# One PSUM tile of eight banks with the kernel's own lists, and an output projection in row halves, in a pre-LayerNorm attention and SwiGLU block

## The chip, the core and the metric

The kernel runs on one core of one Trainium2 chip. The core has a matrix engine (TensorE, in the profile PE for matmuls and PEld for weight loads), a vector engine (VectorE, DVE), a scalar engine (ScalarE, ACT), a general engine (GpSimd, POOL) and a queue that issues transfers (SyncE, SP). Matmul results land in PSUM, which has 128 partitions and eight banks of 512 float32 values per partition; VectorE and ScalarE read them out. The metric is the device time of one execution in microseconds, lower is better.

## The reference

One sequence of 2048 tokens and 640 channels goes through attention with 32 heads of 20 channels and through a SwiGLU feed-forward with 1728 hidden units; both have a LayerNorm without weights in front and a residual around.

```python
def _A_ref(x, wqkv, wo):
    qkv = ((x @ wqkv).reshape(B, S, 3, H, Dh)).transpose(2, 0, 3, 1, 4)
    q, k, v = qkv[0], qkv[1], qkv[2]
    scores = jnp.einsum("bhqd,bhkd->bhqk", q, k) * (Dh ** -0.5)
    p = _softmax(scores, axis=-1)
    o = jnp.einsum("bhqk,bhkd->bhqd", p, v)
    return o.transpose(0, 2, 1, 3).reshape(B, S, D) @ wo
def _B_ref(x, w_gate, w_up, w_down):
    return (_silu(x @ w_gate) * (x @ w_up)) @ w_down
h  = x + _A_ref(_layernorm(x), A_wqkv, A_wo)
h2 = h + _B_ref(_layernorm(h), B_w_gate, B_w_up, B_w_down)
```

## The kernel before

The program is one straight list of instructions, unrolled in Python. The order on each engine is the order in which the code calls them; a framework adds the waits between engines. Most float32 operands are split into a high and a low part (`split`, line 87: a copy on ScalarE, a subtraction on another engine), and a product is taken as hi*hi + hi*lo + lo*hi.

**PSUM.** In each stage the kernel opens a pool of PSUM tiles, and closes it before the next. A pool gives tiles of one name in a ring: the next tile of a name waits until the one that held the same buffer has been read for the last time. The first tiles of a new pool lie where tiles of the old pool lay. The four pools are:

- `psum_f` (line 70), for the first token flips: three `ps_wide` of two banks, one `ps_one`;
- `psum` (line 871), for the input projection: three `ps_one`, five `ps_single`;
- `psum_a` (line 995), for attention: four `ps_one` (scores), three `ps_max`, one `acc`;
- `psum2` (line 1494), for the feed-forward: four `ps_b`, four `ps_a`.

**Stage 1, to 328 us.** Tokens are normalised, transposed by TensorE (`flip_tokens`, line 759, and `flip`, line 739) and multiplied with wqkv. The first two blocks of output (`first_blocks`, line 781; products at line 788) use whole 128-row products. All later ones run as jobs of a planner (`Halves`, line 514): a job goes through its 15 products once with the upper 64 rows of the contraction and once with the lower 64 (`issue`, line 547; products at 556), so two jobs can use the two row halves of the array at the same time. In between it places products for the maxima of the scores (lines 186 and 210). The planner keeps its own clock and reckons when banks come free; its order does not depend on the profile.

**Stage 2, 328 to 1470 us: attention.** A unit is one group of four heads and one chunk of 512 queries; there are 32 (`NU`), 0 to 31, and each has 16 steps `kt`, one for each 128 keys. A step follows a string such as `"sMsSmSmW"` (line 43). `s` and `S` are score products, in the lower and upper row half (`scores`, line 1331, product 1336, exponential by ScalarE at 1342). `m` and `M` are products for the maxima of later units, again in row halves (`max_one`, line 225, product 229, reduced by VectorE at 235). `W` weighs the values with the exponentials of the step before (`weigh`, line 1344, product 1346, into `acc`, in column tiles of 32); after it, one entry of the list `extra` is run. When no maxima are left, the string is `"sSsSW"`. At the end of a unit `acc` is copied out (`row_sums`, line 1354, copy at 1356).

The output projection is cut by query chunk (`projection`, line 1038). In the last two units, 30 and 31, `extra` holds the projection of chunk 0 and of chunk 1: in steps 0 to 7 one half-projection each (`project`, line 1063: 15 products of 128 rows at line 1070 into one bank of `ps_max`, added to h by VectorE at line 1076, statistics at 1077 and 1079), in steps 8 to 10 the LayerNorm factors, in steps 12 to 15 a transpose with its split (`flip`, line 1095, products at 1102). Chunks 2 and 3 are projected after attention, from `ps_b`.

**Stage 3, 1470 us to the end.** Projections 2 and 3, and the feed-forward: `products` (line 1510, product 1514) into `ps_a`, and the down projection (`multiply`, line 1605, product 1608) into `ps_b`.

## Time and profile before

| what | value |
|---|---|
| time, median of 3 runs | 2038.6 us (2038.28 to 2039.58) |
| the profiled execution's own time | 2035.66 us |
| its span, first to last instruction | 2033.9 us |
| mean granted TensorE clock | 0.997 |
| PE busy, PEld busy | 99%, 61% of the span |
| DVE, ACT, POOL busy | 79%, 72%, 39% |

A row of the profile in order of time gives the start and duration in microseconds, the engine, the line, the operation, the tile written and those read, and the shape; in square brackets stands how long the engine was idle before, and what ended that. Matmuls are pipelined and their ends are modelled, so rows of PE overlap, and a busy PE is not PE at its peak. `L88` and `L89` are the two halves of the helper `split`.

### The profile page before, as it was taken

Reading aid. Unit: us, or ns where it says so; the run is one execution under the profiler, and the core shown is the slowest. Engines: PE = TensorE matmul, PEld = TensorE weight load, DVE = VectorE, ACT = ScalarE, POOL = GpSimd, SP = SyncE. Lnnn points to the kernel's source line nnn. Section 1 sums busy time; section 2 is a strip of 40 time slices with the busy share of each in tenths; the row PEclk is TensorE's granted clock in tenths of the full one; section 3 lists DMA queues with packets and bytes.
Section 4 is the critical chain, followed back from the end, with each engine's and each line's share of the span. In section 5 each row is a group of like instructions: output and inputs, shape, how many; then the busy total and the mean of one; then the engine's idle time right before and its main releaser. Section 6 shows DMA issues by size and latency. Waiting matters only on the chain. (4 is left out here: it accounts for less than half of the span.)

```text
span 2033.9 us, 39129 instructions
## 1 busy us (share of the span) xinstructions
PE 2008.8 (99%) x13716; PEld 1238.9 (61%) x13716; DVE 1612.6 (79%) x3241; ACT 1462.4 (72%) x2952; POOL 785.7 (39%) x1079
## 2 busy tenths in 40 slices
PE   7999999999999999999999999999999999999999
PEld 6899996333333333333333333345598888888888
DVE  6678788888888888888888888885377666676677
ACT  3788988999999999999999999987633222211221
POOL 5554450334434334344430011011145454744555
PEclk9999999999999999999999999999999999999999
DMA  7776663343443534444433123211158654974642
GB/s 227 243 222 186 203 185 100 113 128 99 150 124 113 163 123 138 129 141 146 141 126 109 30 65 80 83 62 49 41 193 292 222 193 156 346 272 159 202 151 95
DMA packets 205124, 305.03 MB, mean 150 GB/s; under 512 B 47664, under 2 KB 82480, under 8 KB 203904
## 3 DMA queue, kind: packets, MB, share of 16 engines
q1 hardware_dynamic: 204832, 302.53, 45.9%
q8 instruction: 109, 1.79, 0.4%
q14 instruction: 87, 0.71, 0.1%
q10 hardware_dynamic: 96, 0.00, 0.0%
HBM read 205.78 MB, written 95.68 MB: 148 GB/s over the span
## 5 line engine op out<-in xcount | busy, mean ns | idle before, releaser
L1342 ACT ACTIVATE probs<-ps_one 128x512 f32<-128x512 f32 x2048 | 1056.9, 615 | 62.0 <-PE ps_one L1336 24.2
L235 DVE TENSOR_REDUCE mx<-ps_max 128x1 f32<-128x512 f32 x1472 | 925.4, 684 | 116.2 <-PE ps_max L229 64.1
L1336 PE MATMUL ps_one<-q_stk,k_stk 62*128 62x512 f32 x2048 | 583.5, 431 | 1.2 <-DVE mx L199 1.2
L1346 PE MATMUL acc<-probs,v_stk 128*32 128x512 f32 x4096 | 546.7, 605 | 0.0
L229 PE MATMUL ps_max<-k_stk,q_stk 60*128 60x512 f32 x1472 | 488.7, 440 | 0.1
L1336 PEld LDWEIGHTS ps_one<-q_stk,k_stk 62*128 62x128 f32 x2048 | 290.5, 185 | 284.7 <-ACT probs L1342 269.7
L229 PEld LDWEIGHTS ps_max<-k_stk,q_stk 60*128 60x128 f32 x1472 | 245.2, 185 | 165.4 <-DVE mx L235 126.9
L1729 DVE TENSOR_TENSOR tmp<-ps_a,tmp 128x512 f32<-128x512 f32 x208 | 141.3, 690 | 122.1 <-PE ps_a L1514 96.4
L1346 PEld LDWEIGHTS acc<-probs,v_stk 128*32 128x32 f32 x4096 | 80.6, 108 | 181.7 <-issue 169.5
L1608 PE MATMUL ps_b<-halves,yp 128*128 128x320 f32 x1032 | 179.0, 308 | 1.5 <-POOL yp L89 1.3
L1608 PEld LDWEIGHTS ps_b<-halves,yp 128*128 128x128 f32 x1032 | 165.2, 188 | 17.5 <-POOL yp L89 1.5
L1514 PE MATMUL ps_a<-t,units 128*128 128x512 f32 x624 | 162.5, 396 | 0.0
L246 POOL CAST both<-neg 128x16 fp32r<-128x16 f32 x32 | 6.6, 207 | 361.6 <-PE ps_one L1336 153.7
L1514 PE MATMUL ps_a<-z,units 128*128 128x512 f32 x516 | 133.9, 394 | 0.0
L89 POOL TENSOR_TENSOR yp<-y,yp 128x256 fp32r<-128x256 f32 x96 | 60.2, 627 | 189.8 <-ACT yp L88 189.8
L1514 PEld LDWEIGHTS ps_a<-t,units 128*128 128x128 f32 x624 | 112.6, 188 | 18.5
L1613 DVE TENSOR_TENSOR h<-ps_b,h 128x320 f32<-128x320 f32 x248 | 110.0, 482 | 6.9 <-PE ps_b L1608 5.4
L216 DVE CUSTOM_DVE_ANT_0 q_stk<-ps_single,q_stk 128x512 f32<-128x512 f32 x143 | 95.7, 689 | 22.4 <-ACT q_stk L222 15.0
L1514 PEld LDWEIGHTS ps_a<-z,units 128*128 128x128 f32 x516 | 93.1, 187 | 16.0
L556 PE MATMUL ps_one<-z_hi,w_hi 64*128 64x512 f32 x380 | 99.1, 402 | 1.8 <-ACT z_hi L88 1.7
L88 ACT ACTIVATE yp<-tmp 128x512 fp32r<-128x512 f32 x40 | 25.3, 632 | 103.2 <-POOL tmp L1601 103.2
L1381 POOL TENSOR_TENSOR o<-o,rb 128x512 f32<-128x512 f32 x31 | 39.9, 1286 | 152.9 <-ACT probs L1342 55.8
(221 smaller groups left out, 3017.9 us busy)
## 6 DMA issues: line engine op xcount, KB each, us to landing
units<-w_d SPq DMA_DIRECT2D x186, 256.0 KB
w_d<-stage SPq DMA_DIRECT2D x106, 256.0 KB
halves<-j_d SPq DMA_DIRECT2D x70, 320.0 KB
k_stk<-qk_d SPq DMA_DIRECT2D x112, 160.0 KB
j_d<-stage SPq DMA_DIRECT2D x42, 320.0 KB
q_stk<-qk_d SPq DMA_DIRECT2D x64, 160.0 KB
k_stk<-qk_d SPq DMA_DIRECT2D x112, 80.0 KB
rb<-r_d SPq DMA_DIRECT2D x32, 256.0 KB
```

The source lines that it names most:

```text
L89: lo_engine.tensor_tensor(out=lo, in0=src, in1=hi.bitcast(F32), op=ALU.subtract)
L216: nc.vector.tensor_tensor_reduce(out=place, in0=pss[1], in1=place, scale=1.0, scalar=LEAST, op0=ALU.add, op1=ALU.max, accum_out=mx[:, b, p ...
L229: nc.tensor.matmul(ps, queries[u][rows, pair, t * P : (t + 1) * P], keys[u // NC][rows, pair, kc * CH : (kc + 1) * CH], start=True, stop=True,
L235: nc.vector.tensor_reduce(mxs[u][:, b, pair, t, kc : kc + 1], ps, axis=AX.X, op=ALU.max)
L556: product = nc.tensor.matmul(job["ps"][:, :out], lhs, rhs, start=(half == 0 and i == 0), stop=(half == 1 and i == job["n"] - 1),)
L1336: nc.tensor.matmul(ps, keys[u // NC][rows, p, kt * P : (kt + 1) * P], queries[u][rows, p, :], start=True, stop=True,)
L1342: nc.scalar.activation(probs[p][:, b, :], ps, AF.Exp, scale=scale)
L1346: nc.tensor.matmul(acc[32 * j : 32 * j + 32, :], values[u // NC][:, kt, j * VW : j * VW + 32], probs[j // 2][:, j % 2, :], start=(kt == 0) ...
L1514: nc.tensor.matmul(ps.rearrange("p (t n) -> p t n", t=TPC), w[k][:, i], z[k][:, :, j], start=(first and m == 0), stop=(last and m == len(n ...
L1608: nc.tensor.matmul(ps, a, b, start=(n == 0), stop=(n == len(pairs) - 1))
L1613: nc.vector.tensor_tensor(out=h, in0=ps, in1=h, op=ALU.add)
L1729: add = lambda out, ps, x: nc.vector.tensor_tensor(out=out, in0=ps, in1=x, op=ALU.add)
```

## The change

One PSUM tile of all eight banks is allocated for the whole kernel. A function `turn` gives out its banks in order from a list of places, and each kind of use has such a list. Between stages nothing is closed: the lists are regrouped. In stage 1 a job takes its bank out of the list and puts it back at its end. Waits now come from the banks themselves.

In addition, projections 0 and 1 (units 30 and 31) run in row halves: each of the 15 products becomes two of 64 rows into two banks, and VectorE adds both to h, one after the other. For the transposes of chunk 1 the copy of the split moves from ScalarE to VectorE; chunk 0 keeps it on ScalarE. In unit 31, except in its last step, the weighing is done for two steps at a time, in every second step.

```diff
+    psum = ctx.enter_context(tc.tile_pool(name="psum", bufs=1, space=bass.MemoryType.PSUM))
+    banks = psum.tile([P, 8, CH], F32, name="banks")
+    wide_places, one_places, single_places = [2, 4, 6], [0, 1, 2], [3, 4, 5, 6, 7]
+    def turn(places):
+        places.append(places.pop(0))
+        return places[-1]
     def ps_wide():
-        return psum.tile([P, 2, CH], F32, name="ps_wide", tag="ps_wide", bufs=wides)
+        i = turn(wide_places)
+        return banks[:, i : i + 2]
     def ps_one():
-        return psum.tile([P, CH], F32, name="ps_one", tag="ps_one", bufs=ones)
+        return banks[:, turn(one_places)]
...
-                    job["ps"] = ps_one()
+                    job["place"] = one_places.pop(0)
+                    job["ps"] = banks[:, job["place"]]
...
+                    one_places.append(job["place"])
...
-    ps_ctx.close()
-    ps_ctx = ExitStack()
-    psum = ps_ctx.enter_context(tc.tile_pool(name="psum_a", bufs=1, space=bass.MemoryType.PSUM))
...
+    a, b, c, *max_places = single_places
+    one_places.append(b)
+    max_places, acc_place = [a, c, max_places[0]], max_places[1]
     def ps_max():
-        return psum.tile([P, CH], F32, name="ps_max", tag="ps_max", bufs=3)
+        return banks[:, turn(max_places)]
...
-            ps = ps_of()
+            rows = [slice(b * ROW, (b + 1) * ROW) for b in range(2)] if halved else [slice(0, P)]
+            pss = [ps_of() for _ in rows]
...
+                    for r, ps in zip(rows, pss):
+                        nc.tensor.matmul(
+                            ps[:, :HALF], a[r, k, :], w[r, k, hs],
+                            start=(n == 0), stop=(n == 3 * ND - 1),
+                        )
...
-            nc.vector.tensor_tensor(out=h, in0=ps[:, :HALF], in1=h, op=ALU.add)
+            for ps in pss:
+                nc.vector.tensor_tensor(out=h, in0=ps[:, :HALF], in1=h, op=ALU.add)
...
+                if c == 0:
+                    split(src, hi, lo, nc.vector)
+                else:
+                    nc.vector.tensor_copy(hi, src)
+                    nc.vector.tensor_tensor(out=lo, in0=src, in1=hi.bitcast(F32), op=ALU.subtract)
...
-                    if todo:
-                        weigh_next()
+                    both = u == NU - 1 and kt < NT - 1
+                    for _ in range(2 * (1 - kt % 2) if both else 1):
+                        if todo:
+                            weigh_next()
...
-                        c - 1, ps_max if c < NC - 1 else (lambda: ps_b())
+                        c - 1, *((ps_max, True) if c < NC - 1 else (lambda: ps_b(),))
...
-    ps_ctx.close()
-    psum2 = ctx.enter_context(tc.tile_pool(name="psum2", bufs=1, space=bass.MemoryType.PSUM))
+    max_places.append(acc_place)
     def ps_b():
-        return psum2.tile([P, CH], F32, name="ps_b", tag="ps_b", bufs=4)
+        return banks[:, turn(one_places)]
     def bank():
-        return psum2.tile([P, CH], F32, name="ps_a", tag="ps_a", bufs=4)
+        return banks[:, turn(max_places)]
```

More of the change, by code (lines that the diff above doesn't have):

```diff
@@ L68, in tile_block @@
     const = ctx.enter_context(tc.tile_pool(name="const", bufs=1))
-    ps_ctx = ExitStack()
-    psum = ps_ctx.enter_context(tc.tile_pool(name="psum_f", bufs=1, space=bass.MemoryType.PSUM))
-    wides, ones = 3, 1
+    psum = ctx.enter_context(tc.tile_pool(name="psum", bufs=1, space=bass.MemoryType.PSUM))
[4 more added lines that the diff above has]
+        return places[-1]
     def ps_wide():
-        return psum.tile([P, 2, CH], F32, name="ps_wide", tag="ps_wide", bufs=wides)
+        i = turn(wide_places)
+        return banks[:, i : i + 2]
     def ps_one():
-        return psum.tile([P, CH], F32, name="ps_one", tag="ps_one", bufs=ones)
+        return banks[:, turn(one_places)]
     def ps_single():
-        return psum.tile([P, CH], F32, name="ps_single", tag="ps_single", bufs=5)
+        return banks[:, turn(single_places)]
     ident = const.tile([P, P], F32, name="ident")
@@ L1036, in split_wo, with projection @@
         nc.gpsimd.tensor_tensor(out=lo, in0=raw, in1=hi.bitcast(F32), op=ALU.subtract)
-    def projection(c, ps_of):
+    def projection(c, ps_of, halved=False):
         loaded, zs = {}, {}
@@ L1107, in flip @@
                     dst = both_of(z2_c[c])[:, :, t]
[L1108 removed]
+                    hi, lo = dst[:, :, 0], dst[:, :, 1]
                 else:
                     dst = rest_of(z2_c[c])[:, t]
[L1111 removed]
+                    src, hi, lo = ps[:, :P], dst[:, 0], dst[:, 1]
+                if c == 0:
[3 more added lines that the diff above has]
+                    nc.vector.tensor_tensor(out=lo, in0=src, in1=hi.bitcast(F32), op=ALU.subtract)
         def first(t, half):
@@ L1407, in weigh_next @@
         if kt == 0:
-            accs[u] = psum.tile([P, CH], F32, name="acc", tag="acc", bufs=1)
+            accs[u] = banks[:, acc_place]
         weigh(u, kt, probs, accs[u])
```

13 lines of the change are left out of this document (removed).

## The prediction

> **What bounds the kernel now.** I read the profile in this order: the busy shares, the same by stage (windows), the waits, and the order of time where one stage meets the next.
>
> ```profile
> span 2033.9 us, 39129 instructions
> ...
> 400.00:800.00 400.00, 400.00 (x2812) 156.83 (x2806) 355.50 (x584) 389.86 (x771) 153.84 (x286) 1.00 0.41 128
> 1361.70:1398.96 37.26, 37.26 (x244) 23.80 (x240) 22.31 (x45) 19.20 (x37) 5.98 (x4) 1.00 0.26 83
> 1418.61:1449.63 31.02, 31.02 (x208) 20.86 (x204) 7.75 (x18) 17.97 (x35) 5.96 (x4) 1.00 0.20 57
> 1449.63:1470.88 21.25, 20.51 (x126) 7.41 (x125) 10.05 (x26) 19.96 (x42) 1.55 (x1) 1.00 0.01 1
> ```
>
> After the window and its length, the columns are PE, PEld, DVE, ACT, POOL, then clock, DMA share, GB/s. In the middle of attention (second row) ScalarE's exponentials fill 97% of the time; nothing of the change acts there. In the last two units it is another stage: where projections run (third and fourth row) ScalarE is busy only 52% and 58%, so PE and what it waits for set the pace; in the last row ScalarE is back at 94%. The sum therefore has five places: three seams between stages and two units.
>
> **Seam 1, token flips to the first blocks.** These rows are the end of the old pool and the first product of the new one.
>
> ```profile
> 14.39 2.50 DVE L89 TENSOR_TENSOR z_lo<-ps_wide,z_hi 128x640 fp32r<-128x640 f32 x3
> ...
> 15.33 0.70 ACT L88 ACTIVATE z_hi<-ps_wide 128x640 fp32r<-128x640 f32 x1 [0.53 <-PE ps_wide L763]
> ...
> 16.95 2.56 PE L788 MATMUL ps_one<-z_hi,w_hi 128*128 128x512 f32 x10 [1.65 <-DVE z_lo L89]
> ```
>
> The first ten products read only z_hi, ready at 16.03, and wait for z_lo (16.89) because it reads the old pool. In the new lists the flips use banks 4, 6, 2, 4 and the blocks banks 0 and 1, so they start at about 16.08: 0.9 us earlier. z_lo is needed ten products (2.2 us) later and is there. Bounds 0 to -0.9 (later waits on VectorE could swallow it); I take -0.9, since work behind it is queued on PE's results.
>
> **Seam 2, last maximum products to attention.**
>
> ```profile
> 325.48 1.81 ACT L197 ACTIVATE q_stk<-ps_single 128x256 f32<-128x256 f32 x6
> ...
> 328.10 0.18 PEld L1336 LDWEIGHTS ps_one<-q_stk,k_stk 62*128 62x128 f32 x1 [1.54 <-DVE mx L199]
> ...
> 328.69 4.03 ACT L1342 ACTIVATE probs<-ps_one 128x512 f32<-128x512 f32 x8 [1.39 <-PE ps_max L229]
> ...
> 331.85 0.20 PEld L1346 LDWEIGHTS acc<-probs,v_stk 128*32 128x32 f32 x8 [0.65 <-issue]
> ...
> 337.75 0.16 PEld L1346 LDWEIGHTS acc<-probs,v_stk 128*32 128x32 f32 x8 [0.37 <-issue]
> ...
> 339.88 0.16 PEld L1346 LDWEIGHTS acc<-probs,v_stk 128*32 128x32 f32 x8 [0.37 <-issue]
> ```
>
> The first score waits for VectorE's last reduction although three of its four banks were never in that reduction's list. With lists the scores follow the last maximum product, and the first exponential follows ScalarE's last copy (327.29) instead of 328.69: -1.3 us, bounds 0 (SBUF of the closing pool may hold it) to -1.4.
>
> ```profile
> 52.00:56.00 4.00, 4.00 (x25) 3.84 (x23) 1.55 (x8) 2.94 (x8) 4.00 (x4) 0.57 0.65 179
> ...
> 328.00:329.00 1.00, 0.90 (x6) 0.79 (x7) 0.38 (x3) 0.31 (x1) 0.00 (x0) 0.82 0.00 0
> 335.00:336.00 1.00, 1.00 (x7) 0.22 (x9) 1.00 (x3) 0.78 (x3) 0.00 (x0) 0.77 0.00 0
> ```
>
> Behind this gap the clock runs at half: 0.82 in 328 to 329 means it fell at 328.64; 0.77 in 335 to 336 means it came back at 335.46. Two weighings apart (331.85 to 337.75) took 5.90 us where 2 x 2.13 (337.75 to 339.88) is 4.26, so 1.6 us were lost there, and some 0.7 in the four exponentials (2.06) and one score (0.4) between 328.69 and 331.85: 2.3 us. With scores in the gap I take the half-speed stretch as gone: -2.3; bounds -2.3 and 0. [...]
>
> **Seam 3, attention to the third projection.**
>
> ```profile
> 1468.59 1.55 PE L1346 MATMUL acc<-probs,v_stk 128*32 128x512 f32 x8
> ...
> 1470.23 0.60 ACT L1356 ACTIVATE o<-acc 128x512 f32<-128x512 f32 x1 [0.52 <-issue]
> ...
> 1470.88 0.74 PEld L1070 LDWEIGHTS ps_b<-wo_hi,o_hi 128*128 128x128 f32 x5 [1.65 <-ACT o L1356]
> ```
>
> The projection waits for the copy of acc, whose bank it doesn't use. With lists it starts when the weighing ends, 1470.1: -0.8 (bounds 0 to -0.8). PE has no gap in the 18 us behind, so it passes on.
>
> **Unit 30: projection 0 in row halves, beside maximum products.**
>
> ```profile
> 1361.70 0.74 PEld L1070 LDWEIGHTS ps_max<-wo_hi,o_hi 128*128 128x128 f32 x5 [0.84 <-DVE mx L235]
> ...
> 1366.41 0.74 PEld L1070 LDWEIGHTS ps_max<-wo_hi,o_hi 128*128 128x128 f32 x5 [0.84 <-DVE mx L235]
> ...
> 1367.99 0.90 PE L1070 MATMUL ps_max<-wo_hi,o_lo 128*128 128x320 f32 x5
> 1368.81 0.18 PEld L229 LDWEIGHTS ps_max<-k_stk,q_stk 60*128 60x128 f32 x1 [0.19 <-issue]
> ...
> 1368.92 0.49 DVE L1076 TENSOR_TENSOR h<-ps_max,h 128x320 f32<-128x320 f32 x1 [1.91 <-PE ps_max L1070]
> ...
> 1369.45 0.49 DVE L1077 BATCH_NORM_STATS2 st<-h 128x6 f32<-128x320 f32 x1
> 1369.46 0.18 PEld L229 LDWEIGHTS ps_max<-k_stk,q_stk 60*128 60x128 f32 x1 [0.36 <-DVE h L1076]
> ...
> 1370.10 1.83 DVE L235 TENSOR_REDUCE mx<-ps_max 128x1 f32<-128x512 f32 x3
> 1370.13 0.16 PEld L1346 LDWEIGHTS acc<-probs,v_stk 128*32 128x32 f32 x8 [0.37 <-issue]
> ...
> 1394.25 0.74 PEld L1070 LDWEIGHTS ps_max<-wo_hi,o_hi 128*128 128x128 f32 x5 [0.84 <-DVE mx L235]
> ```
>
> Seven steps between the first and the last of eight half-projections took 32.55 us, 4.65 each. One is 15 products at 0.147 (five end in 0.90, each 0.31 long) and costs 2.40 from load to load (1366.41 to 1368.81); 0.19 of it is the idle "issue" where the tile shape changes from 128 rows to the scores' 64. Row halves remove that: -0.19. But a step now takes five banks from a list of three (two halves, three maximum products) where it took four. Count from the first add. It frees its bank after 0.54 (1368.92 to 1369.46). The second add reads what the first wrote, as the statistics do, so it starts at 0.53 and frees its bank at 1.07. The third maximum product needs that one: 0.53 later than now. Statistics start at 1.06, the reductions 0.65 behind them at 1.71 (1369.45 to 1370.10; 0.2 less in every other step, without the aggregate), each 0.61. The next projection's second half takes the second maximum product's bank, free at 1.71 + 1.22 + 0.05 = 2.98. PE itself would be there at 2.73 (weighing at 1370.13, 0.53 later, and 0.99 of weighing, from 1421.72 to 1422.71 below), so the bank decides. Then 0.11 of load, 14 x 0.147, the last product 0.31 and 0.03: the next add at 5.49, or 5.28 without the aggregate, mean 5.38. Price: 7 x 0.73 and 0.3 behind the last one, +5.4. Bounds: -1.5 (eight shape changes saved, no bank wait) and +6.5 (0.2 more a step, if the second add is released as late as a reduction). [...]
>
> **Unit 31: projection 1 in halves, no maximum products, two weighings at a time.**
>
> ```profile
> 1421.72 0.16 PEld L1346 LDWEIGHTS acc<-probs,v_stk 128*32 128x32 f32 x8 [0.39 <-issue]
> ...
> 1422.71 0.74 PEld L1070 LDWEIGHTS ps_max<-wo_hi,o_hi 128*128 128x128 f32 x5 [0.84 <-DVE st L1077]
> ...
> 1425.11 0.30 PEld L1336 LDWEIGHTS ps_one<-q_stk,k_stk 62*128 62x128 f32 x4 [0.19 <-issue]
> ...
> 1425.81 0.16 PEld L1346 LDWEIGHTS acc<-probs,v_stk 128*32 128x32 f32 x8 [0.39 <-issue]
> ...
> 1450.19 10.21 ACT L1342 ACTIVATE probs<-ps_one 128x512 f32<-128x512 f32 x20 [2.02 <-PE ps_one L1336]
> ```
>
> Now a step is 0.99 + 2.40 + 0.70 = 4.09. Two steps become: scores 0.46 and projection 2.21 without a shape change; then scores 0.70, two weighings 1.84 (0.99 and 0.85; 0.80 if only the change of shape is saved, 0.99 if nothing), projection 2.21. The odd step is 2.67, the even 4.75. Steps 1 to 7 (four odd, three even) take 24.9 instead of 28.6, and the step before saves 0.19: -3.9. Here five calls don't meet in three banks, and VectorE has 1.5 us of work a step. From step 8 on, 20 exponentials run without a gap (10.21). Two weighings (1.84), 0.43 of score before and 0.56 behind are 2.83 against the 2.04 of four exponentials: ScalarE then starves by some 0.8 at three places, less 0.4 at the first, where it starts behind: +2.0. The flips' copies go from ScalarE to VectorE, which is half idle there (10.05 of 21.25); PE's shape changes and the chain of copy and subtraction take their place: 0. Net -1.9, bounds -4.5 (no starving) and 0.
>
> Lists instead of rings elsewhere: same number of banks for each kind in every stage, same order: 0, bounded by the 51 ns of a wait instruction that PE's queue hides.
>
> **Sum:** -0.9 - 1.3 - 2.3 - 0.8 + 5.4 - 1.9 = -1.8. The profiled execution took 2035.66 (span 2033.9), 2.9 under the median of the runs; against it the sum is 2033.9, against the median of 2038.6 it is **2036.8**. What a measurement can tell from no change is 0.2%, 4.1 us.
>
> **Rivals.** (1) The banks don't bind in unit 30: VectorE is busy 22.31 of 37.26 there, so it has room, if its order doesn't matter. Then -1.5 stands for +5.4: 2029.9. Against it: the 0.36 of waiting for the add that is there already. (2) The half-speed stretch stays: 2039.1; for it, that the drain before 326 is thin in any case. (3) Slower: the pairs of halves don't hide their weight loads.
>
> ```profile
> 317.77 0.31 PE L556 MATMUL ps_one<-w_hi,z_lo 64*128 64x320 f32 x1
> 317.83 0.31 PE L556 MATMUL ps_one<-w_hi,z_hi 64*128 64x320 f32 x1
> 317.83 0.18 PEld L556 LDWEIGHTS ps_one<-w_hi,z_hi 64*128 64x128 f32 x1
> 317.92 0.31 PE L556 MATMUL ps_one<-w_hi,z_lo 64*128 64x320 f32 x1
> ```
>
> A load lasts 0.18; if pairs go at that pace, 16 x 15 x 0.035 = +8.4: 2045.2, slower from 0.024 a pair on. Against it, one half steps here from 317.77 to 317.92 in 0.15 with the other beside it. (4) One tile makes waits wider than the bank: each score behind the last exponential would add a microsecond in each of 512 steps, far above 2100; no row speaks for it.
>
> **How the numbers follow.** Forecast 0.36, alone 2033 to 2041; rival 1 0.26, rival 2 0.16, rival 3 0.17, rival 4 0.05. Faster is rival 1 and the lower end of the forecast, 0.27; slower is 3, 4 and the upper end of 2, 0.27; the rest, 0.46, is within. The range, 2030 to 2045, ends at rivals 1 and 3.
>
> **What would show it.** Right: L788 starts near 16.1; no half clock behind 326; L1070 of ps_b right behind acc; in unit 30 the second half's load waits for mx L235 and steps last 5.4; in unit 31 steps of 2.7 and 4.75 alternate, then gaps of 0.8 before exponentials. The prediction is wrong if unit 30's steps stay under 4.7, or if half-projections last longer than 2.3.

## The result: slower by 0.3%, and the profile after

The kernel after takes 2045.7 us (median of 13 executions, 2040.2 to 2049.0), the kernel before 2038.7 (13 executions, 2035.6 to 2043.6). The ratio is 1.0029, with a 95% interval of 1.0020 to 1.0039. Forecast was 2036.8. The profiled execution of the kernel after took 2047.7 us (span 2045.8), 2.0 over its median; that of the kernel before lay 3.1 under its own. So the 11.9 us between the two spans overstate the difference, and single marks must be read with that in mind.

These rows of the view by windows answer to those shown of before (columns as there): a microsecond behind seam 2, the middle of attention, unit 30 from its first half-projection to that of unit 31, unit 31 from its first half-projection to the end of its eighth, and the rest of unit 31 up to the third projection.

```profile
333.00:334.00 1.00, 1.00 (x5) 0.42 (x4) 1.00 (x3) 0.74 (x2) 0.00 (x0) 0.50 0.75 185
...
400.00:800.00 400.00, 400.00 (x2813) 157.05 (x2809) 355.05 (x584) 389.79 (x771) 153.14 (x285) 1.00 0.42 129
1365.19:1427.79 62.60, 59.93 (x486) 32.70 (x483) 38.84 (x83) 38.85 (x78) 8.51 (x7) 1.00 0.16 51
1427.79:1456.14 28.35, 28.35 (x319) 21.51 (x317) 11.19 (x25) 18.07 (x35) 5.97 (x4) 1.00 0.17 47
1456.14:1479.97 23.83, 22.96 (x139) 8.22 (x135) 12.41 (x33) 16.82 (x33) 1.55 (x1) 0.93 0.07 20
```

Behind seam 2 the clock runs at half again. The middle is untouched: ScalarE is busy 389.79 us of 400 as before (389.86). Unit 30 takes 62.60 us where it took 56.91 before (1361.70 to 1418.61). Unit 31's first part is 2.7 us shorter (28.35 for 31.02), and its rest 2.6 us longer (23.83 for 21.25), with ScalarE busy 71% instead of 94% and a granted clock of 0.93.

The view in order of time gives the places where stages meet and the first step of unit 30:

```profile
15.90 0.70 ACT L94 ACTIVATE z_hi<-banks 128x640 fp32r<-128x640 f32 x1 [0.53 <-PE banks L771]
16.66 2.55 PE L796 MATMUL banks<-z_hi,w_hi 128*128 128x512 f32 x10 [0.79 <-ACT z_hi L94]
...
330.36 0.18 PEld L1344 LDWEIGHTS banks<-q_stk,k_stk 62*128 62x128 f32 x1
...
331.19 2.56 ACT L1350 ACTIVATE probs<-banks 128x512 f32<-128x512 f32 x5
...
331.94 3.67 DVE L241 TENSOR_REDUCE mx<-banks 128x1 f32<-128x512 f32 x6
332.68 0.18 PEld L235 LDWEIGHTS banks<-k_stk,q_stk 60*128 60x128 f32 x1 [0.66 <-DVE mx L241]
...
341.37 0.16 PEld L1354 LDWEIGHTS banks<-probs,v_stk 128*32 128x32 f32 x8 [0.36 <-issue]
...
1365.19 0.74 PEld L1072 LDWEIGHTS banks<-wo_hi,o_hi 64*128 64x128 f32 x10 [0.84 <-DVE mx L241]
...
1367.35 0.18 PEld L235 LDWEIGHTS banks<-k_stk,q_stk 60*128 60x128 f32 x1
...
1367.69 1.09 DVE L1079 TENSOR_TENSOR h<-banks,h 128x320 f32<-128x320 f32 x2 [2.45 <-PE banks L1072]
...
1368.24 0.18 PEld L235 LDWEIGHTS banks<-k_stk,q_stk 60*128 60x128 f32 x1 [0.70 <-DVE h L1079]
...
1368.83 0.18 PEld L235 LDWEIGHTS banks<-k_stk,q_stk 60*128 60x128 f32 x1 [0.41 <-DVE h L1079]
...
1369.49 0.16 PEld L1354 LDWEIGHTS banks<-probs,v_stk 128*32 128x32 f32 x8 [0.37 <-ACT probs L1350]
...
1370.49 0.79 PEld L1072 LDWEIGHTS banks<-wo_hi,o_hi 64*128 64x128 f32 x10 [0.84 <-DVE mx L241]
...
1402.82 0.79 PEld L1072 LDWEIGHTS banks<-wo_hi,o_hi 64*128 64x128 f32 x10 [0.84 <-DVE mx L241]
...
1430.84 0.73 PEld L1072 LDWEIGHTS banks<-wo_hi,o_hi 64*128 64x128 f32 x9 [0.32 <-DVE h L1079]
...
1479.97 0.74 PEld L1072 LDWEIGHTS banks<-wo_hi,o_hi 128*128 128x128 f32 x5 [0.84 <-issue]
```

What is to be seen: at all three seams the product starts where the prediction put it. The first blocks follow z_hi and no longer z_lo. The first score comes with the last maximum product of stage 1 (whose load is at 330.35), and the third projection follows the last weighing. In unit 30, though, two maximum products now wait for additions on VectorE, 0.70 and 0.41 us in one step, where before one waited 0.36. In unit 31 (1430.84) a half's second load waits 0.32 us for an addition.

The table follows marks through both profiles, in microseconds.

| mark | before | after | difference |
|---|---|---|---|
| first block product (its flips 0.57 later in this execution) | 16.95 | 16.66 | -0.3 |
| third weighing of attention | 337.75 | 341.37 | +3.6 |
| unit 30, first half-projection | 1361.70 | 1365.19 | +3.5 |
| unit 31, first half-projection | 1418.61 | 1427.79 | +9.2 |
| third projection | 1470.88 | 1479.97 | +9.1 |
| end of span | 2033.9 | 2045.8 | +11.9 |

The first 3.6 us arise in stage 1 and at seam 2, partly from half-speed stretches of the clock, which lie elsewhere in every execution (here from 70.0 and from 332.9 us, 6.83 us each; in the profile of before 3.41 us from 52.2 and 6.83 from 328.6). The next 5.7 arise in unit 30, 5.1 of them between its first and its last half-projection (37.63 us for 32.55). Unit 31 gives nothing in sum. Of the last 2.8, 0.8 arise within 20 us of the third projection, 0.8 between 1520 and 1540 us and 1.3 behind the last addition; the experiments come back to the last two.

### The profile page after: what moved, and what is told of

Same layout as the page of the kernel before. It is cut to its first block, busy times and chain, and to the rows that moved or that the text cites. A ratio compares the mean times of both kernels' runs of the same rounds, so it can differ in the third digit from the quotient of the medians.

```text
span 2045.8 us, 39488 instructions
## 1 busy us (share of the span) xinstructions
PE 2014.5 (98%) x13956; PEld 1242.0 (61%) x13956; DVE 1624.5 (79%) x3265; ACT 1461.1 (71%) x2944; POOL 785.6 (38%) x1079
## 5 line engine op out<-in xcount | busy, mean ns | idle before, releaser
L1350 ACT ACTIVATE probs<-banks 128x512 f32<-128x512 f32 x2048 | 1057.2, 615 | 68.8 <-PE banks L1344 37.8
L241 DVE TENSOR_REDUCE mx<-banks 128x1 f32<-128x512 f32 x1472 | 924.9, 684 | 116.4 <-PE banks L235 63.9
L1344 PE MATMUL banks<-q_stk,k_stk 62*128 62x512 f32 x2048 | 584.6, 430 | 0.7 <-ACT probs L1350 0.7
L1354 PE MATMUL banks<-probs,v_stk 128*32 128x512 f32 x4096 | 546.4, 607 | 0.0
L235 PE MATMUL banks<-k_stk,q_stk 60*128 60x512 f32 x1472 | 490.7, 440 | 2.9 <-DVE h L1079 1.6
L1344 PEld LDWEIGHTS banks<-q_stk,k_stk 62*128 62x128 f32 x2048 | 291.8, 185 | 282.2 <-ACT probs L1350 269.0
L235 PEld LDWEIGHTS banks<-k_stk,q_stk 60*128 60x128 f32 x1472 | 245.3, 185 | 171.3 <-DVE mx L241 127.6
L1616 PE MATMUL banks<-halves,yp 128*128 128x320 f32 x1032 | 179.0, 308 | 1.5 <-DMA halves<-j_d 1.3
L1616 PEld LDWEIGHTS banks<-halves,yp 128*128 128x128 f32 x1032 | 165.2, 188 | 17.5 <-POOL yp L95 1.5
L1522 PE MATMUL banks<-t,units 128*128 128x512 f32 x624 | 162.5, 396 | 0.0
```

The costliest lines, as they stand in the source:

```text
L235: nc.tensor.matmul(ps, queries[u][rows, pair, t * P : (t + 1) * P], keys[u // NC][rows, pair, kc * CH : (kc + 1) * CH], start=True, stop=True,
L241: nc.vector.tensor_reduce(mxs[u][:, b, pair, t, kc : kc + 1], ps, axis=AX.X, op=ALU.max)
L1344: nc.tensor.matmul(ps, keys[u // NC][rows, p, kt * P : (kt + 1) * P], queries[u][rows, p, :], start=True, stop=True,)
L1350: nc.scalar.activation(probs[p][:, b, :], ps, AF.Exp, scale=scale)
L1354: nc.tensor.matmul(acc[32 * j : 32 * j + 32, :], values[u // NC][:, kt, j * VW : j * VW + 32], probs[j // 2][:, j % 2, :], start=(kt == 0) ...
L1522: nc.tensor.matmul(ps.rearrange("p (t n) -> p t n", t=TPC), w[k][:, i], z[k][:, :, j], start=(first and m == 0), stop=(last and m == len(n ...
```

## The experiments

The theory after this reading: unit 30's row halves cost 5.7 us because of the banks; in unit 31 the halves gain and the weighing in pairs loses it; and the lists' earlier starts at the seams are given back at the next wait. The rival: the lists themselves slow stage 1. All kernels are compared with the kernel before, run on the same chip (its median there is 2038.3 to 2039.1 us in the timed comparisons, its clock 0.9969 to 0.9972). The clock is the mean granted clock over the timed executions.

| kernel | median us | ratio (95%) | clock |
|---|---|---|---|
| after | 2045.7 | 1.0029 (1.0020 to 1.0039) | 0.9969 |
| lists only | 2039.6 | 1.0007 (0.9998 to 1.0016) | 0.9979 |
| unit 30 whole | 2038.7 | 1.0001 (0.9992 to 1.0010) | 0.9979 |
| single weighing | 2043.5 | 1.0030 (1.0018 to 1.0042) | 0.9968 |
| base: unit 30 whole, single weighing | 2037.9 | 0.9998 (0.9988 to 1.0007) | 0.9972 |
| base, pairs to step 8 | 2036.7 | 0.9985 (0.9975 to 0.9995) | 0.9975 |
| base, z_lo first | 2035.7 | 0.9986 (0.9977 to 0.9995) | 0.9975 |
| base, six more products | 2034.7 | 0.9979 (0.9971 to 0.9988) | 0.9986 |
| base, all three | 2035.4 | 0.9982 (0.9973 to 0.9992) | 0.9982 |
| base, all three, halves in unit 30, lent bank | 2042.6 | 1.0020 (1.0011 to 1.0030) | 0.9977 |
| after, with a lent bank in unit 30 | 2046.9 | 1.0042 (1.0029 to 1.0054) | 0.9959 |

What the units take is steadier than the medians. From the loads that begin each unit's projections (the kind of row shown above), in microseconds; "unit 30" runs to unit 31's first half-projection, "unit 31" from there to the third projection:

| kernel | unit 30 | unit 31 |
|---|---|---|
| before | 56.91 | 52.27 |
| after | 62.60 | 52.18 |
| lists only | 57.00 | 51.40 |
| unit 30 whole | 56.98 | 52.48 |
| single weighing | 62.60 | 48.40 |
| base | 56.97 | 48.42 |
| base, flips' copy on ScalarE | 56.95 | 49.63 |
| base, pairs to step 8 | 57.02 | 48.31 |
| after, with a lent bank in unit 30 | 62.91 | 54.17 |
| base, all three, halves in unit 30, lent bank | 62.94 | 48.32 |

**The lists alone.** The projections are whole, weighings single, and the flips' copy is back on ScalarE.

```diff
-                        c - 1, *((ps_max, True) if c < NC - 1 else (lambda: ps_b(),))
+                        c - 1, *((ps_max, False) if c < NC - 1 else (lambda: ps_b(),))
...
-                    both = u == NU - 1 and kt < NT - 1
+                    both = False
...
-                if c == 0:
-                    split(src, hi, lo, nc.vector)
-                else:
-                    nc.vector.tensor_copy(hi, src)
-                    nc.vector.tensor_tensor(out=lo, in0=src, in1=hi.bitcast(F32), op=ALU.subtract)
+                split(src, hi, lo, nc.vector)
```

> Left of the change: the lists alone (projections in whole rows, one weighing a step, the flips' copy on ScalarE as before). Theory A (the slower unit 30 and the half-speed stretches make the loss, the lists themselves gain): the three seams give 0.9, 1.2 and 0.8 us, so the kernel takes about 2.9 us less than before, 2035 to 2038 where before has 2038.7; unit 30's steps are 4.65 us, unit 31's 4.09, and the third projection starts right behind the last weighing. Theory B (the lists move stage 1's order of work against the transfers, and that makes the loss): still 2040 or more, with TensorE idle for about 3 us at 67 us, as in the profile after the change.

Measured: 1.0007, so neither theory's time is met: 1.4 us above before where 2.9 below were expected, the interval holding zero. Units 30 and 31 behave as expected (57.00 and 51.40, the 0.9 of seam 3 in the latter). TensorE's wait at 67 us is there, as the rival had it. Where the other seams' gain goes is seen in the next three fences. First, TensorE's waits from 60 to 76 us with the lists alone:

```profile
PE banks L563 <- POOL z_lo L95: 2.9, 1, 2.9
PE banks L563 <- ACT z_hi L94: 0.7, 1, 0.7
```

and seam 3 in order of time, same kernel: 

```profile
1470.21 0.73 PEld L1072 LDWEIGHTS banks<-wo_hi,o_hi 128*128 128x128 f32 x5 [0.84 <-issue]
...
1477.71 0.74 ACT L94 ACTIVATE o_hi<-o_t 128x640 fp32r<-128x640 f32 x1 [4.48 <-DMA o_t<-o_d]
...
1480.64 0.74 PEld L1072 LDWEIGHTS banks<-wo_hi,o_lo 128*128 128x128 f32 x5 [0.16 <-POOL o_lo L95]
...
1485.70 0.45 PEld L1072 LDWEIGHTS banks<-wo_hi,o_lo 128*128 128x128 f32 x3 [0.66 <-POOL o_lo L95]
```

The third projection starts 0.8 us earlier against its surroundings (1470.21, everything else standing 0.14 later than in the profile of before), and loses 0.82 again in two waits within 16 us: o_lo is made from o_hi, and o_hi waits for the load of o_t. The products ran ahead of the transfers.

**The kernel before once more**, for another profile of its first stage.

> The kernel before, unchanged, for another profile of its first stage. Theory A (the longer wait at 67 to 70 us comes with the lists): as in its first profile, GpSimd's subtraction on k_stk starts at about 65.6 us after 3.8 us of waiting, and TensorE waits 0.5 us for z_lo. Theory B (transfers scatter that much by themselves): the wait is 1.5 to 3 us here too.

The waits of TensorE from 60 to 76 us, and the windows behind 71 and 334 us, of the kernel before in this second execution:

```profile
PE ps_one L556 <- POOL z_lo L89: 2.3, 1, 2.3
PE ps_one L556 <- ACT z_hi L88: 0.7, 1, 0.7
```

```profile
72.00:75.00 3.00, 2.98 (x17) 2.27 (x15) 0.78 (x4) 0.90 (x3) 0.60 (x1) 0.50 0.77 239
335.00:338.00 3.00, 3.00 (x13) 0.69 (x15) 1.51 (x3) 1.88 (x4) 0.00 (x0) 0.50 0.33 107
```

Theory B holds: the kernel before has the long wait and the half-speed stretch behind it too. The first profile of before, with 0.5 us of waiting, was the exception. Aligned instruction by instruction, this second execution of before stands 3.9 us behind the first at 100 us (0.9 of it from the start), the kernel after 2.9. So the rival (the lists slow stage 1) falls as a cause of the 7 us.

**z_lo first.** This restores the wait of seam 1; it is made on the base of the table, the kernel with lists, halves in unit 31 only and single weighings. (The order of the sum's terms in the first blocks differs.)

```diff
-            for n, (a, w) in enumerate(((z_hi, w_hi), (z_lo, w_hi), (z_hi, w_lo))):
+            for n, (a, w) in enumerate(((z_lo, w_hi), (z_hi, w_hi), (z_hi, w_lo))):
```

> The same kernel as with single weighings and halves in unit 31, but the first ten products of the first blocks read z_lo instead of z_hi, so that they wait for it as before the change and start near 16.95 us instead of 16.1. Theory A (the 0.9 us of seam 1 are given back at 65 to 70 us, where GpSimd's next z_lo stands behind a subtraction that waits for a transfer): TensorE's wait for GpSimd at 67 to 70 us is shorter by 0.5 us or more, and everything from 80 us on stands where it stood, within 0.4 us, once half-speed stretches are set off. Theory B (the gain of seam 1 lasts): all is 0.9 us later from 80 us on.

VectorE's and ScalarE's instructions stand 1.36 us later than in the base from 21 to 66 us (0.49 of it from the executions' starts), 0.80 later from 69 to 72, and 0.13 earlier from 73 on. TensorE's wait for z_lo is 1.4 us instead of 2.0:

```profile
PE banks L563 <- POOL z_lo L95: 1.4, 2, 0.9
PE banks L563 <- ACT z_hi L94: 0.7, 1, 0.7
```

So 0.56 of the 0.87 us go in that wait, and 0.31 are left (0.80 less the 0.49 of the start). The next 0.93 fall together with a half-speed stretch that the base had at 69.7 us and this execution had not; whether the later start has a part in that, two executions can't tell. Theory A holds within its 0.4 us at 73 us, if the whole 0.93 is the stretch's. Further on this execution gains more against the base, 0.6 us by 200 us and 1.3 by the end of stage 1, and what makes that is open. The times don't show a lasting gain of the earlier start either: 0.9986 with the wait restored, 0.9998 without, and the intervals overlap.

**Unit 30 in whole rows**, all else as changed. `True` becomes `c == 2` in the call of `projection`: chunk 1 keeps its halves, chunk 0 doesn't.

> Projection 0 (unit 30) in whole rows again, all else as changed. Theory A (five calls meet three banks in unit 30): its steps go from 5.38 back to 4.65 us, the unit is 5.7 us shorter, and the time is 5 to 6 us under that of the changed kernel: 2039.5 to 2041. Theory B (unit 30's steps are longer for another reason, such as the second addition on VectorE): less than 3 us are won.

Measured 1.0001 against 1.0029: the 0.0028 are 5.7 us, and by the trace the unit is 5.62 us shorter (56.98). Theory A holds, and its time, 2039.5 to 2041, was missed only to the good side. This is where the change loses.

**A lent bank.** The changed kernel, with one of the four score banks given to unit 30's products for that unit.

```diff
+        if u == NU - 2:
+            max_places.append(one_places.pop(0))
+        if u == NU - 1:
+            one_places.append(max_places.pop(0))
```

> The changed kernel, with one of the four score banks lent to the products of unit 30 for that unit, so that five calls a step meet four banks. Theory A (the bank decides in unit 30): the steps fall from 5.38 us to between 4.45 and 4.75, the unit is 4.5 to 6.5 us shorter, and the time is that much under the changed kernel's 2045.7: 2039 to 2041. Theory B (the second addition and its place on VectorE make the step long, whatever the banks): steps stay above 5.1 us. Theory C (three banks for the scores starve ScalarE): steps of projections shorten, but the steps behind the eight projections in unit 30 get longer, and less than 3 us are won.

In order of time, the first half-projection of unit 30, a score and a maximum product that wait in its midst, the last half-projection, and unit 31's first:

```profile
1365.25 0.74 PEld L1072 LDWEIGHTS banks<-wo_hi,o_hi 64*128 64x128 f32 x10 [0.84 <-issue]
...
1378.40 0.18 PEld L1344 LDWEIGHTS banks<-q_stk,k_stk 62*128 62x128 f32 x1 [0.66 <-ACT probs L1350]
...
1382.88 0.18 PEld L235 LDWEIGHTS banks<-k_stk,q_stk 60*128 60x128 f32 x1 [0.55 <-DVE h L1079]
...
1399.65 0.74 PEld L1072 LDWEIGHTS banks<-wo_hi,o_hi 64*128 64x128 f32 x10 [0.84 <-DVE mx L241]
...
1428.16 0.73 PEld L1072 LDWEIGHTS banks<-wo_hi,o_hi 64*128 64x128 f32 x10 [0.84 <-DVE z L95]
```

Seven steps take 34.40 us, 4.91 each instead of 5.38, so one more bank takes off 0.47 of the 0.73 that a step had lost: the banks do decide most of it. But five calls still meet four banks (0.55 of waiting for the addition), the scores wait for theirs (0.66 for an exponential), and the stretch behind the last half-projection takes 28.51 instead of 24.97 us. In sum the unit is no shorter (62.91): theory C. Eight banks are simply all in use there.

**Single weighing**, both projections in halves, all else as changed (`both = False`).

> One weighing a step in unit 31 again, both projections in row halves, all else as changed. Theory A (weighing in pairs starves ScalarE from step 8 on and leaves TensorE so thin that its clock is halved at 1462.7 us): with single weighings the four pairs of steps take 7.8 us as now (3.9 each), the gaps before exponentials behind step 8 and the half-speed stretch there go, and the time from step 8 to the third projection falls from 23.8 to about 20.5 us: 2.5 to 3.5 us under the changed kernel, 2042 to 2043. Theory B (the pairs save what they were counted at, 0.85 us in two steps): steps of 3.9 cost about as much as the gaps, no difference within 1 us.

By the trace theory A holds and more: unit 31 takes 48.40 instead of 52.18 us. Eight half-projections go at 3.86 each, and from the last of them to the third projection there are 21.41 us instead of 26.36. In the kernel after, ScalarE's view at that place shows the hole, and the clock behind it:

```profile
1464.79 0.50 PEld L1344 LDWEIGHTS banks<-q_stk,k_stk 62*128 62x128 f32 x4 [1.66 <-issue]
...
1465.62 4.03 ACT L1350 ACTIVATE probs<-banks 128x512 f32<-128x512 f32 x8 [2.23 <-PE banks L1344]
```

```profile
1463.00:1464.00 1.00, 1.00 (x12) 0.12 (x4) 0.00 (x0) 0.39 (x1) 0.00 (x0) 0.50 0.00 0
```

With single weighings ScalarE runs through (unit 30 whole, single weighing, in order of time):

```profile
1446.76 10.21 ACT L1350 ACTIVATE probs<-banks 128x512 f32<-128x512 f32 x20 [1.78 <-PE banks L1344]
```

The medians are less clear: 2.1 us under the kernel after, but the same ratio (1.0030 with 5 executions, 2.4 us of uncertainty either way). One part of the 3.8 us is known to be given back: from 1495 to 1510 us this kernel loses 1.1 us against before and the kernel after none, ScalarE again waiting for a load of o_t before its o_hi (4.51 us at 1498.8). The rest is within the uncertainty of the medians.

**Unit 30 whole and single weighing** together.

> Projection 0 in whole rows, projection 1 in row halves, one weighing a step: what is left are the lists, the halves of unit 31 and the flips' copy on VectorE. Theory A: the lists' 2.9 us and eight steps of unit 31 shorter by 0.19 us (1.5 us), so 4.4 us under before: 2033 to 2036, the fastest of the four. Theory B (halves gain nothing even where banks are free): no difference from the lists alone within 0.7 us.

Measured 0.9998, 0.0009 or 1.8 us under the lists alone; expected were 1.5 under them. The intervals overlap (to 1.0007 here, from 0.9998 there), but by the trace unit 31 is 3.0 us shorter (48.42 for 51.40), so theory B falls. Theory A's absolute time, 2033 to 2036, was missed, since the lists alone take no less than before.

**The flips' copy back on ScalarE** (the same kernel, with the last edit of the first diff).

> Lists, halves in unit 31 and single weighings, with the flips' copy back on ScalarE. Theory A (the copy on VectorE is worth 1.2 us, because ScalarE is the bound behind step 8 of unit 31): from the last half-projection to the third projection 22.6 us instead of 21.4. Theory B (as on record, worth nothing): 21.4 us again, and the difference to the lists alone comes from the halves.

Last half-projection at 1448.20, third projection:

```profile
1470.81 0.74 PEld L1072 LDWEIGHTS banks<-wo_hi,o_hi 128*128 128x128 f32 x5 [0.84 <-issue]
```

That is 22.61 us, for 21.41 with the copy on VectorE: theory A. The copy is worth 1.2 us, and the halves the other 1.8 of unit 31's 3.0 (51.40 to 48.40).

**Pairs to step 8** (`both = u == NU - 1 and kt < 9`).

> Lists, halves in unit 31 only, and weighings in pairs only as far as step 8 of unit 31 (single from step 9 on); beside it stands the same kernel with single weighings throughout (2037.9). Theory A (pairs help while the projection runs and harm behind it, where ScalarE sets the pace): steps 0 to 7 of unit 31 take 25.8 us as in the changed kernel instead of 27.0, the time from step 8 to the third projection stays near 21.4, so about 0.8 us are won. Theory B (one pair is enough to starve ScalarE and to bring the half-speed stretch at about 1460 us): 1 us or more is lost.

Between the first and the last half-projection stand 25.86 us instead of 27.01, and behind it 22.45 instead of 21.41. That is no saving: a step without a weighing and one with two take 2.54 and 5.22 us, 7.76 together, and two steps with one each 7.72. The seven steps hold four short ones and three long ones, and the weighing that is owed stands behind the last half-projection. Unit 31 takes 48.31 instead of 48.42, so neither theory's time is met by the trace (0.8 won or 1 lost); the medians' intervals overlap. There was no half-speed stretch in unit 31 here nor in the two other profiles with pairs to step 8, and none in the ten without pairs; all three with pairs throughout had one or two.

**Six more products** at the start of attention (they only repeat scores; their result is overwritten).

```diff
+    def idle_products(kt, n):
+        for _ in range(n):
+            nc.tensor.matmul(
+                banks[:, acc_place],
+                keys[0][0 : NPART + 2, 0, kt * P : (kt + 1) * P],
+                queries[0][0 : NPART + 2, 0, :],
+                start=True, stop=True,
+            )
...
                     scores(u, kt, heads[op == "S"].pop(0), probs)
+                    if now[0] < 2:
+                        idle_products(kt, {(0, 5): 2, (1, 0): 2, (1, 3): 1, (1, 6): 1}.get((kt, at_op), 0))
```

> The same kernel with six more products of 62 rows and 512 columns in the first two steps of attention (they repeat the score product of their step into the bank of the weighted sum, which the first weighing overwrites), at places where TensorE waits. Theory A (TensorE's clock is halved after a window of 3.41 us with too few columns streamed; with 1536 more of half height the windows at 325 to 333 us reach 1100 a microsecond and more): no half-speed stretch between 326 and 345 us, and the third weighing stands where it stands in the executions without such a stretch; the median falls by up to 2 us, as far as executions had the stretch. Theory B (what decides is something else, such as the length of one idle time): the stretch comes in the same share of executions, and the six products cost up to 1.4 us.

Windows around the seam (clock in the third column from the end):

```profile
325.00:328.00 3.00, 2.72 (x12) 1.03 (x9) 2.74 (x15) 2.95 (x10) 0.00 (x0) 1.00 0.33 131
328.00:331.00 3.00, 2.84 (x18) 1.98 (x22) 3.00 (x7) 2.73 (x6) 0.00 (x0) 1.00 0.44 127
331.00:334.00 3.00, 3.00 (x25) 1.04 (x19) 2.53 (x5) 2.42 (x6) 0.00 (x0) 1.00 0.36 102
334.00:337.00 3.00, 3.00 (x22) 1.31 (x20) 2.50 (x5) 2.93 (x7) 0.00 (x0) 1.00 0.00 0
```

No half speed. From the first exponential (327.27) to the third weighing (334.93) are 7.66 us; the base without a stretch has 7.59 (328.40 to 335.99), the kernel after with one 10.18. So the six products cost less than 0.1 us, and a stretch of 6.83 us costs 2.6. One profile without a stretch proves little, since three of the thirteen without the six products have none there either. The mean clock says more: over eleven executions it is 0.9986, against 0.9972 in the base's twelve, and the ratio falls to 0.9979. Theory A is borne out by these, but not in every execution, as the last kernel shows.

**The three together** (z_lo first, pairs to step 8, six products), and **with halves in unit 30 and the lent bank** on top.

> Lists, halves in unit 31 only, pairs of weighings as far as step 8, z_lo first in the first blocks, and the six more products in attention's first two steps. Theory A (each part's gain stands for itself): 0.5 to 1.5 us under the kernel with the six products alone (0.9979 of before), so 0.9972 to 0.9977 of before; no half-speed stretch between 326 and 345 us. Theory B (what one part gains is given back at the next wait): 0.9979 or more.

> As combined, and projection 0 in row halves too, with the lent bank in unit 30. Theory A (with enough banks halves save their 0.19 us a step there as well): unit 30's steps of 4.45 to 4.6 us against 4.65, 0.5 to 1.5 us under combined. Theory B (the fourth bank only removes the loss): the same as combined within 0.5 us, or up to 1 us more.

Together they are no better than the six products alone (0.9982 for 0.9979): theory B. With halves in unit 30 the time is back at 1.0020: the unit takes 62.94 us even with the bank. In that execution the clock was halved at 331.7 us for 10.24 us in spite of the six products.

**VectorE beside GpSimd at 1525 us.** In every kernel with lists 0.7 to 0.8 us are lost between 1520 and 1540 us (less in the second kernel below), and nothing in the second profile of before. Two rows of before and two of the lists alone, in order of time:

```profile
1525.13 0.61 DVE L1861 TENSOR_SCALAR z<-h,mvs,r_late 128x640 f32<-128x640 f32 x1
...
1525.19 1.69 POOL L89 TENSOR_TENSOR halves<-zz,halves 128x512 fp32r<-128x512 f32 x1 [1.03 <-ACT halves L88]
```

```profile
1525.46 1.64 DVE L1865 TENSOR_SCALAR z<-h,mvs,r_late 128x640 f32<-128x640 f32 x1
1525.46 1.29 POOL L95 TENSOR_TENSOR halves<-zz,halves 128x512 fp32r<-128x512 f32 x1 [0.97 <-ACT halves L94]
```

The same normalisation lasts 0.61 or 1.64 us. With lists GpSimd's operand is ready 0.06 us sooner, since a transpose before it starts 0.06 sooner, and the two operations begin together (1525.46). Two kernels, both the lists alone with one subtraction in `flip` moved to VectorE, tried it; the first moved that of chunk 2, the second that of chunk 3.

```diff
-            keep(x, z_d[c - 2], t)
+            if (c, t) == (3, 0):
+                keep(x, z_d[c - 2], t, nc.vector)
+            else:
+                keep(x, z_d[c - 2], t)
```

> The lists alone, and in the first flip of chunk 2 behind attention the subtraction of the halves done by VectorE instead of GpSimd, so that the two engines don't meet at 1525 us. In all profiles with lists VectorE's normalisation (640 elements) lasts 1.64 us there, starting with or just after GpSimd's subtraction; in both of the kernel before it starts 0.06 us ahead of it and lasts 0.61 us; and from 1520 to 1540 us the kernels with lists lose 0.7 us. Theory A (the meeting with GpSimd makes the 0.7 us): the normalisation lasts 0.61 us, and less than 0.4 us are lost from 1520 to 1540 us. Theory B (something else there does): still 0.6 us or more.

> As the run before, but with the right flip: in that one VectorE took over the subtraction of chunk 2's flip, and the meeting with GpSimd's subtraction of chunk 3's remained (1.10 us). Now VectorE does that of chunk 3, behind its own normalisation. Theory A: the normalisation lasts 0.61 us and less than 0.4 us are lost from 1520 to 1540 us against the kernel before. Theory B: still 0.6 us or more.

The first told nothing: it was the wrong flip, the meeting stayed (1.10 us), 0.8 us were lost. In the second:

```profile
1521.82 0.60 DVE L1865 TENSOR_SCALAR z<-h,mvs,r_late 128x640 f32<-128x640 f32 x1
1522.34 0.28 DVE L95 TENSOR_TENSOR kept<-banks,kept 128x128 fp32r<-128x128 f32 x1
1522.54 0.68 DVE L95 TENSOR_TENSOR halves<-zz,halves 128x512 fp32r<-128x512 f32 x1
```

The normalisation lasts 0.60 us and some 0.35 are lost instead of 0.7: theory A. That the rest is the 0.68 of the subtraction on VectorE is not tested.

**Behind the last addition.** No experiment was made for one more loss, which every kernel with lists has. From the end of VectorE's last addition to the end of the span are 3.32 us in both profiles of before, and 4.09 to 5.05 (4.6 on average) in the fourteen others. The result is stored there. Two views of the transfers, in each the busy tenths of the transfer engines in 40 slices and one row of a queue (packets, megabytes, share of the sixteen engines): the kernel before from 2024.7 us to its end, and the lists alone from 2025.7.

```profile
DMA  0001999999999999999999999999999970000000
q1 hardware_dynamic: 1152, 2.62, 73.5%
```

```profile
DMA  0009999992000999999999999999998000000000
q8 instruction: 1, 0.02, 1.0%
```

With lists the transfer engines stand idle for about a microsecond amid the stores. The longest of SyncE's eight store issues lasts 0.54 to 1.48 us in the fourteen kernels, where all last 0.34 at most in the kernel before, and it ends 0.2 to 0.5 us after the last transfer on the queue that the profile calls "instruction". With lists that transfer ends 2 to 4 us ahead of the last addition, in the two profiles of before 18 and 19 us ahead. That it holds the issue up is argued from this order and not tested; why it comes later with lists is open.

## Why the prediction was wrong, step by step

The prediction said 2036.8 us, with a range up to 2045; it came to 2045.7, the slower side. By its own steps:

- **Unit 30, +5.4: right.** Seven steps of 5.38 us were forecast, and 37.63 / 7 = 5.38 were measured; the unit lost 5.7. The mechanism was right (five calls on three banks: the unit alone made whole again wins 5.7 us back, and a fourth bank 0.47 of the 0.73 a step), the waits were divided wrongly. The count let the third maximum product wait for the second addition; in fact the second one waits for the first addition as well (0.70 and 0.41). The second half's wait for a reduction, which was to decide, shows in only two of eight steps (0.29 and 0.33). A step is 2.16 of projection, 1.48 to the third maximum product, 0.66 to the weighing and 1.00 of weighing, with up to half a microsecond of the latter wait on top. Rival 1 (banks don't bind) is refuted.
- **Seams with the half-speed stretch, -5.3 in all: wrong, and this is the step that failed.** Each start came where it was put (0.87, 1.3 and 0.8 us earlier), and the lists alone, where these gains stand without the rest of the change, are 1.4 us slower than before, with zero in the interval. Seam 1's reason, "work behind it is queued on PE's results", fails at 67 us, where the same work waits 2.9 us for GpSimd, which has waited 7.0 for a transfer (both in the kernel after and with the lists alone). Most of seam 2's gain goes by the third weighing: from the first exponential to it are 10.18 us instead of 9.06, and one maximum product alone waits 0.66 for VectorE; the half-speed stretch, which lies 4 us later than before, may have a part in it. Seam 3's "PE has no gap in the 18 us behind, so it passes on" overlooked the operands: the second o_hi comes no earlier (1477.74 us before; 1477.71 with the lists alone, where it waits for the load of o_t), and PE, started 0.8 us earlier, waits 0.82 us for o_lo.
- **The half-speed stretch, -2.3: sized about right, but it didn't go.** Rival 2 describes what happened: with scores in the gap it came all the same, at 332.9 us, and so in eight of the eleven profiles with lists and without the six products. Measured by VectorE's instructions from 320 to 345 us against the first profile of before, the four with lists and a stretch of 6.83 us win 0.0 to 0.4, those with one of 3.41 win 1.4, those without 2.9 to 3.0, and the second profile of before loses 0.5. The prediction took one profile's stretches as the state before; they are a draw for each execution.
- **Lists instead of rings elsewhere, 0: wrong, about +2.0.** The number of banks and the order are the same, as the prediction says, but the 0.06 us at 1525 us cost 0.75, and behind the last addition 1.3 more are lost. Taken off the lists' +1.4, these leave about -0.6 for the seams and the stretch together; that is an estimate, with 1.8 us of uncertainty either way from the interval of the lists alone.
- **Unit 31 and seam 3, -2.7: wrong, -0.1.** "Five calls don't meet in three banks" is true, four do: the odd step's second half waits for the first addition (0.32 us), so two steps take 7.75 instead of 7.42, and with single weighings they take 7.72: the pairs save nothing. From step 8 on the pairs cost more than 2.0: ScalarE's gaps are 2.23 and 0.99 us rather than 0.8, the first of them inside a half-speed stretch that follows the thinner work. The flips' copy, counted at 0, is worth 1.2. Without the pairs the unit gives 3.8 (52.27 to 48.42), of which 0.9 are seam 3's.
- **Rivals 3 and 4: refuted.** Ten loads in halves take 0.74 us and a half-projection 2.16 (2.40 before); ScalarE's share in the middle is unchanged.

So the sum missed because every gain was credited up to the end of the kernel, the lists' own cost was put at nothing, and the one loss, sized well, was all that was left. By ratios: +1.4 for the lists, +5.7 for unit 30, and about -1.2 left for unit 31, to make 5.9 (0.0029 of 2038.7). The last of these is not firm: by the traces unit 31 with all its changes is 1.1 us longer than with the lists alone (52.48 for 51.40), and the intervals hold both.

The kernel with lists, halves in unit 31 only, single weighings and six more products beats both: 0.9979 of before (0.9971 to 0.9988), 4.4 us. It is the best of several, and its interval ends where that of the base begins.

## What to carry to other kernels

A product that starts earlier gains only up to the next thing that comes by its own timetable (of seam 1's 0.87 us, 0.56 went in one wait); before crediting it, follow the operands of the next 20 us back to their transfers and to the queue of the engine that prepares them, for an engine without gaps may be just behind its loads. Follow the kernel to the end of its span, too: here a microsecond went behind the last arithmetic, where no term of the sum looked. Splitting the product over row halves took two banks here where one had done, and with five calls on three banks a step went from 4.65 to 5.38 us: count calls against banks in every step, each with the addition that frees it, before counting what the split saves. And take more than one profile of the kernel before where the clock drops: the first one here was 3 us better than usual in places the change had nothing to do with.

## What the runs showed of the hardware

**The clock.** All half-speed stretches that end within the span are multiples of 3.41 us (3.41, 6.83 and 10.24), and within a trace they lie on one grid (in the kernel after the starts are 77 and 331 times 3.4133 apart), whose phase is another in every execution (the first grid point after the span's start lies at 0.96 us in the first profile of before, at 1.78 in that of after). A measure for each window of the grid, in all sixteen traces from 15 to 2025 us, is the sum of the columns that the products streamed, each weighted with its tile's share of the array. Of some 9300 windows at full clock with at least 950 columns a microsecond none was followed by a half-speed window; of 79 with fewer, 29 were (the most in any window is 2260). Which of those it is, the measure doesn't tell: in the kernel after half speed followed a window of 826 columns a microsecond (from 329.46 us) and none followed one of 721 (from 1466.09), and most windows under 870 that had no such consequence lie at 1405 to 1470 us, where weighings in 32-column tiles count for a quarter. One of the 29 shows TensorE at work: from 1459.27 to 1462.68 matmuls filled 87% of the window (643 columns a microsecond), and half speed came at 1462.68.

**VectorE and GpSimd.** An operation of VectorE that lasted 0.61 us when it began 0.06 us ahead of GpSimd's (which then lasted 1.69) lasted 1.64 when the two began together (GpSimd's 1.29); so 0.06 us of earlier readiness cost 0.7 us. In the first of the two kernels above it began 0.54 us behind GpSimd's, at 1529.80, and lasted 1.10. Both times it ended 0.35 us after GpSimd's (1527.10 and 1526.75, 1530.90 and 1530.55), and 1.64 is 0.26 less than the two durations added (1.90). What holds either up beside the other, no row shows.
